# Attention with one product per head: each head on its own half of TensorE's rows, in a fused attention and two-layer expert kernel

## The chip, the core and the metric

The kernel runs on one core of a Trainium2 chip. The metric is device microseconds of one execution; the median of three runs of the kernel before is 1247.96 us (1246.36 to 1250.62). TensorE is called PE here (its weight loads are PEld), VectorE DVE, ScalarE ACT, GpSimd POOL, and SyncE's DMA queue SP.

## What is computed

```python
def _attn_ref(q, k, v, alpha):                       # B, H, S, D = 4, 8, 768, 48
    state = np.zeros((B, H, D, D))
    for t in range(S):
        state = alpha[:, :, t, :, None] * state + np.einsum('bhd,bhe->bhde', k[:, :, t], v[:, :, t])
        y[:, :, t] = np.einsum('bhd,bhde->bhe', q[:, :, t], state)
...
x = attn_out.transpose(0, 2, 1, 3).reshape(3072, 384)
x = _moe_ref(x)      # 8 experts, each token goes to the one with the largest cosine, scaled by its gate
return _moe2_ref(x)  # 4 experts, every token through all of them, mixed by domain_probs
```

All inputs are fp32; a head has 48 numbers per token, and the decay alpha is a number per token and per row of the state.

## The kernel before, in words

**Attention** is done in chunks of 128 tokens, all eight heads of a batch row at a time: 24 units, six to each of the four batch rows, three to each of eight loads. The eight heads stand as four pairs p, a pair on 96 partitions (48 rows for each head). Per load (`g`) and half of the pairs (`pp`), DVE computes with a backward scan the decays from each token to the end of its chunk (`G`, `prep1`), their reciprocals, and with a forward scan the inverse decays (`bf`); POOL multiplies them with q and k (`prep2`), so that `bf` becomes the scaled queries and `G` the scaled keys. `bcall` holds the whole decay of a chunk, once for each head of a pair, with zeros (`hmask`) in the other head's rows. `prep3` on ACT writes the queries twice (`qb`), each time with the other head's 48 rows at zero.

A unit u then runs in three steps of the main loop. `S1(u)`: per pair, one product of the 96 key rows with both masked queries (128x256) gives the scores of two heads in `A`; DVE applies the causal mask (`At`); PE transposes the keys (`kn`). `S2(u)`, a step later: scores times values, per head, into `y` (one head in columns 0 to 63 of the array, the other in 64 to 111); the state `S` of the chunks before, per pair, into the same `y`; and `U`, keys times values per pair (96x96, of which the two 48x48 blocks on the diagonal are wanted). DVE adds `U` to the state and scales it by `bcall` (`state`). `S3(u)`, one more step later: `fin` turns `y` into token rows and router scores; DVE reduces the scores (`raw`), ACT takes squares and a copy (`sj`, `xb`).

**Routing** works on groups of units (`groups`): `choose` (5 DVE instructions), ranks by small products on PE (`route_a`), `route_b` and `route_c` (16 more on DVE), scaling on ACT and an indirect DMA per unit from POOL that scatters token rows to expert rows in DRAM (`xs`). Rows of `xs` that no token fills are zeroed ahead (`prefill`).

**The experts** follow: eight routed ones, then four dense ones, as products in split precision on PE (L120 to L122, L208 to L210, L267 to L269). The order of instructions on each engine is the order in which the code is written, and each engine takes its own in order.

Of the kernel before, what the change touches and what calls it, by code (L numbers as in the profile page):

```python
# [7 lines left out]
F32 = mybir.dt.float32  # L8
# [14 lines left out]
NG = 8  # L23
# [3 lines left out]
W0 = max(WIN)  # L27
NR = 3072
AMIN, BMAX, GMIN = 0.75, 1.0e9, 1.0e-20
# [275 lines left out]
def attention_and_routing(tc, a, small, keep, xs, info_d, wst, load_w, split_w):  # L305
# [3 lines left out]
    ends = [4, 8, 12, 16, 20, 22, 24]  # L309
    groups = list(zip([0] + ends[:-1], ends))  # L310
    with ExitStack() as ctx:
        c1 = ctx.enter_context(tc.tile_pool(name="attc", bufs=1))
        tin = ctx.enter_context(tc.tile_pool(name="tin", bufs=3))
# [4 lines left out]
        xbp = ctx.enter_context(tc.tile_pool(name="xbp", bufs=7))  # L318
# [3 lines left out]
        cst = c1.tile([128, 688], F32, name="cst")  # L322
# [4 lines left out]
        sr = cst[0:1, 608:640].rearrange("p (a e) -> p a e", e=8)  # L327
        tri = keep["ti"][:, 0]
        hmask = c1.tile([96, 2], F32, name="hmask")
        tau = c1.tile([128, 1], F32, name="tau")  # L330
        pre = wst.tile([128, 2 * DM], F32, tag="wraw", name="pre")[:, 0:DM]
        dind = c1.tile([96, 774], F32, name="dind")
        dfw = c1.tile([96, 774], F32, name="dfw")
        bcall = c1.tile([96, NG, 3, 4, 2], F32, name="bcall")
        Sb = [c1.tile([96, 4, 112], F32, name=f"S{j}") for j in range(2)]
        aacc = c1.tile([96, NG, 2], F32, name="aacc")
# [4 lines left out]
        srow = c1.tile([1, 4, 8], BF16, name="srow")  # L341
# [7 lines left out]
        tins, vins, qbd, qqs, kts, mid = {}, {}, {}, {}, {}, {}  # L349
# [11 lines left out]
        def prefill(e):  # L361
            nc.sync.dma_start(
                out=xs[e * NR:e * NR + W0, :].rearrange("(p j) d -> p j d", j=4),
                in_=pre[0:112, :].unsqueeze(1).to_broadcast([112, 4, DM]),
            )
# [5 lines left out]
        def prep1(g, pp, c0=0, c1=3, part=2):  # L371
            al = tins[g, pp]
            lo, hi = 2 * CW * c0, 2 * CW * c1
            if c0 == 0 and part != 1:
                mid[g, pp] = [
                    bd.tile([96, 774], F32, tag="G", name="G"), bd.tile([96, 774], F32, tag="bf", name="bf", bufs=6)
                ]
# [31 lines left out]
        def prep3(g, pp, c0=0, c1=3):  # L409
            qq = qqs[g, pp]  # L410
            if c0 == 0:
                qbd[g, pp] = bd.tile([96, 6, 2, 128], F32, tag="qb", name="qb")
            cs = slice(2 * c0, 2 * c1)
            for s in range(2):
                nc.scalar.activation(  # L415
                    out=qbd[g, pp][:, cs, s, :], in_=qq[:, cs], func=AF.Copy, scale=hmask[:, s:s + 1]
                )

        def prep4(g, pp):
            del mid[g, pp]  # L420
            al = tins.pop((g, pp))[:, 0:774]
            junk = ew.tile([96, 6, 128], BF16, tag="ajunk", name="ajunk", bufs=1)
            nc.scalar.activation(
                out=junk, in_=c3(al, CW)[:, :, 1:CW], func=AF.Relu, scale=-1.0, bias=cbias[0:96, :],
                accum_out=aacc[:, g, pp:pp + 1],
            )
# [3 lines left out]
        def S1(u):  # L430
            g, cl = divmod(u, 3)
            At = wk.tile([128, 8, 128], F32, tag="At", name="At")
            for pp in range(2):
                ps = psA.tile([128, 4, 128], F32, tag="A", name="A")
                kt, qb = kts[g, pp], qbd[g, pp]
                for j in range(2):
                    i = 2 * cl + j
                    nc.tensor.matmul(  # L438
                        ps[:, 2 * j:2 * j + 2, :].rearrange("p s w -> p (s w)"),
                        lhsT=kt[:, i, :], rhs=qb[:, i].rearrange("p s w -> p (s w)"),  # L440
                        start=(j == 0), stop=True, skip_group_check=True,
                    )
                nc.vector.tensor_tensor(  # L443
                    out=At[:, 4 * pp:4 * pp + 4, :], in0=ps,
                    in1=tri.unsqueeze(1).to_broadcast([128, 4, 128]), op=ALU.mult,
                )
            Ats[u] = At
            if u % 6 < 5:
                pk = ps1.tile([128, 4, 96], F32, tag="kn", name="kn")
                for p in range(4):  # L450
                    nc.tensor.matmul(
                        pk[:, p, :], lhsT=kts[g, p // 2][:, 2 * cl + p % 2, :], rhs=ident[0:96, 0:96],
                        is_transpose=True, start=(p == 0), stop=True, skip_group_check=True,
                    )
                kn = wk.tile([128, 4, 96], F32, tag="kn", name="kn_s")
# [4 lines left out]

        def halves(t):
            return bass.AP(t.tensor, t.offset, [t.ap[0], t.ap[1], [64, 2], [1, D]])

        def S2(u):
# [4 lines left out]
            for p in range(4):  # L469
                for s in range(2):  # L470
# [4 lines left out]
                        o, lhsT=v[:, cl, c0:c0 + n], rhs=At[:, 2 * p + s, :],  # L475
# [648 lines left out]
```

## Time and profile before

| | before |
|---|---|
| median of three runs | 1247.96 us |
| the profiled execution, its own time | 1249.04 us |
| its span, first to last instruction | 1247.3 us |
| busy: PE, DVE, ACT, POOL | 95%, 34%, 28%, 26% of the span |
| PE matmuls, weight loads | 6565, 6565 |
| mean granted PE clock | 0.977 of full speed |

The shares are averages over two stages that differ: attention with routing takes about the first 200 us, the experts the remaining 1040 us. PE's 95% is made by the second; in the first, several engines share the work, and the limits are read there stretch by stretch. A matmul of fp32 operands shows as two instructions, each with a weight load.

### The profile page before, as it was taken

The page shows a single profiled execution, that of the slowest core. Times are in us where ns is not written, and L with a number is a line of the kernel's source. Part 1 is how long each engine was busy: PE and PEld are TensorE (multiplying, and loading weights), DVE is VectorE, ACT ScalarE, POOL GpSimd, SP SyncE. Part 2 cuts the span into 40 slices and gives each one's busy share as a digit, 9 for nine tenths or more (in the row PEclk, how much of TensorE's full clock was granted, in tenths as well). Part 3 has the DMA queues.
Part 4 walks back from the last instruction along what each step waited for, and adds up shares of the span by engine and source line. Part 5 has one row for each costly group of instructions (what it writes and reads, how often), then busy time and mean ns, then how long its engine had stood idle before and what let it go on. Part 6 is the DMA issues. An engine that isn't in the chain of part 4 may idle for free.

```text
span 1247.3 us, 16110 instructions
## 1 busy us (share of the span) xinstructions
PE 1189.9 (95%) x6565; PEld 1088.5 (87%) x6565; DVE 424.8 (34%) x791; ACT 351.3 (28%) x624; POOL 321.2 (26%) x223
## 2 busy tenths in 40 slices
PE   5978895999999999999999999999999999999996
PEld 4867785999999999999999999999999899999996
DVE  8998965222222212222222222222212222222221
ACT  3556553444444421111221111131111121111111
POOL 4565644566667510000220000040000020111111
PEclk9997887999999999999999999999999999999998
DMA  8945505444443500000120000030000010000000
GB/s 243 278 150 156 154 31 168 143 131 125 137 137 115 130 26 1 1 1 1 39 64 1 1 1 1 1 93 10 1 1 1 1 39 1 26 26 26 26 26 28
DMA packets 31355, 79.08 MB, mean 63 GB/s; under 512 B 7448, under 2 KB 12824, under 8 KB 29928
## 3 DMA queue, kind: packets, MB, share of 16 engines
q1 hardware_dynamic: 27432, 68.43, 19.0%
q0 software_dynamic: 3840, 9.54, 2.1%
q8 instruction: 53, 0.87, 0.3%
q14 instruction: 30, 0.25, 0.1%
HBM read 62.82 MB, written 15.14 MB: 63 GB/s over the span
## 4 chain that ended last, share of the span: by engine, by line
PE 84%; DVE 7%; issue 4%; DMA 1%; POOL 1%; SPq 0%; ACT 0%; POOLq 0%; ACTq 0%
PE h L120 13%; PE h L122 13%; PE h L121 13%; PE p L269 10%; PE p L268 10%; PE p L267 10%; PE o L208 3%; PE o L209 3%; PE o L210 3%; DVE bf L393 1%; PE A L438 1%; DVE G L380 1%; DVE At L443 1%; PE fin L513 1%; PE xt L175 1%
## 5 line engine op out<-in xcount | busy, mean ns | idle before, releaser
L112 DVE SCALAR_TENSOR_TENSOR hl<-h,hh 128x512 fp32r<-128x512 f32 (+8 forms) x264 | 171.9, 651 | 746.5 <-ACT hh L111 746.5
L68 POOL TENSOR_TENSOR wu<-wraw,wu 128x768 fp32r<-128x768 f32 x96 | 178.3, 1859 | 659.6 <-ACT wu L67 651.4
L111 ACT ACTIVATE hh<-h 128x512 fp32r<-128x512 f32 (+8 forms) x264 | 149.5, 566 | 671.2 <-PE h L122 671.2
L269 PE MATMUL p<-wu,hl 128*128 128x384 f32 x768 | 258.8, 337 | 0.0
L268 PE MATMUL p<-wu,hh 128*128 128x384 f32 x768 | 258.2, 336 | 0.0
L267 PE MATMUL p<-wu,hh 128*128 128x384 f32 x768 | 258.1, 336 | 0.0
L120 PE MATMUL h<-x,wu 128*128 128x512 f32 (+1 forms) x600 | 233.0, 388 | 0.0
L122 PE MATMUL h<-x,wu 128*128 128x512 f32 (+1 forms) x600 | 230.6, 384 | 0.0
L121 PE MATMUL h<-x,wu 128*128 128x512 f32 (+1 forms) x600 | 228.0, 380 | 0.0
L268 PEld LDWEIGHTS p<-wu,hh 128*128 128x128 f32 x768 | 144.3, 188 | 7.4
L267 PEld LDWEIGHTS p<-wu,hh 128*128 128x128 f32 x768 | 144.4, 188 | 7.1
L269 PEld LDWEIGHTS p<-wu,hl 128*128 128x128 f32 x768 | 144.3, 188 | 0.0
L122 PEld LDWEIGHTS h<-x,wu 128*128 128x128 f32 x600 | 112.6, 188 | 26.6
L121 PEld LDWEIGHTS h<-x,wu 128*128 128x128 f32 x600 | 112.8, 188 | 16.1
L120 PEld LDWEIGHTS h<-x,wu 128*128 128x128 f32 x600 | 112.8, 188 | 14.5
L67 ACT ACTIVATE wu<-wraw 128x768 fp32r<-128x768 f32 x96 | 80.8, 843 | 76.2 <-PE o L210 38.1
L280 POOL DMA_INDIRECT out_dram<-acc,toki x24 | 23.4, 973 | 183.4 <-DVE acc L276 178.5
L120 PE MATMUL h<-xh,wu 128*128 128x448 f32 (+6 forms) x192 | 70.2, 365 | 0.0
L438 PE MATMUL A<-qb,G 96*128 96x256 f32 x192 | 55.2, 433 | 14.0 <-ACT qb L415 8.4
L121 PE MATMUL h<-xh,wu 128*128 128x448 f32 (+6 forms) x192 | 68.2, 355 | 0.0
L122 PE MATMUL h<-xl,wu 128*128 128x448 f32 (+6 forms) x192 | 68.0, 354 | 0.0
L208 PE MATMUL o<-hh,wu 128*128 128x448 f32 (+6 forms) x192 | 67.7, 352 | 0.0
(150 smaller groups left out, 1170.6 us busy)
## 6 DMA issues: line engine op xcount, KB each, us to landing
wraw<-in_wu_dram SPq DMA_DIRECT2D x96, 384.0 KB, 3.1
tin<-in_aqk_dram SPq DMA_DIRECT2D x14, 866.6 KB, 6.2
xs<-pre SPq DMA_DIRECT2D x8, 672.0 KB, 9.9
xw<-xs SPq DMA_DIRECT2D x7, 672.0 KB, 6.1
v<-in_v_dram SPq DMA_DIRECT2D x8, 576.0 KB, 6.7
tin<-in_aqk_dram SPq DMA_DIRECT2D x2, 384.0 KB, 6.3
xw<-xs SPq DMA_DIRECT2D x3, 224.0 KB, 3.6
tin<-in_aqk_dram SPq DMA_DIRECT2D x2, 193.5 KB, 4.9
```

The lines of the kernel that those rows point to most:

```text
L67: nc.scalar.activation(out=t[:, 0], in_=r, func=AF.Copy)
L68: nc.gpsimd.tensor_tensor(out=t[:, 1], in0=r, in1=t[:, 0].bitcast(F32), op=ALU.subtract)
L111: nc.scalar.activation(out=hh[:, 0:n], in_=ps, func=AF.Relu)
L112: nc.vector.scalar_tensor_tensor(out=hl[:, 0:n], in0=ps, scalar=0.0, in1=hh[:, 0:n].bitcast(F32), op0=ALU.max, op1=ALU.subtract)
L120: nc.tensor.matmul(ps, lhsT=w[:, 0, ks], rhs=xh(k), start=(k == 0), stop=False)
L121: nc.tensor.matmul(ps, lhsT=w[:, 1, ks], rhs=xh(k), start=False, stop=False)
L122: nc.tensor.matmul(ps, lhsT=w[:, 0, ks], rhs=xl(k), start=False, stop=(k == KD - 1))
L208: nc.tensor.matmul(o, lhsT=w[:, 0, ds], rhs=hh[:, 0:n], start=(f == 0), stop=False)
L267: nc.tensor.matmul(o, lhsT=hh[:, js], rhs=w[:, 0, DM:2 * DM], start=(f == 0), stop=False)
L268: nc.tensor.matmul(o, lhsT=hh[:, js], rhs=w[:, 1, DM:2 * DM], start=False, stop=False)
L269: nc.tensor.matmul(o, lhsT=hl[:, js], rhs=w[:, 0, DM:2 * DM], start=False, stop=(f == NFB - 1))
L438: nc.tensor.matmul(ps[:, 2 * j:2 * j + 2, :].rearrange("p s w -> p (s w)"), lhsT=kt[:, i, :], rhs=qb[:, i].rearrange("p s w -> p (s w)"), ...
```

## The change

A pair now stands on partitions 0 to 47 and 64 to 111 (`R = 112`); the 16 rows between are filled once per buffer from a small array (`pad`), and each load of a pair is two DMAs of 48 partitions instead of one of 96. Every head gets a product of its own on its half of the array's rows, for the scores, for the state's part of `y`, and for `U`. Masked queries (`prep3`), the head mask and the zeroed half of the states go; `bcall` is copied by ACT; the state is 112x4x48. Routing groups are six units, three times, and then three of two; `prefill` writes rows 128 to 447 of each expert instead of 0 to 447.

```diff
+LOW = (NT - sum(WIN) + min(WIN)) // 64 * 64
+R = 112
...
-    ends = [4, 8, 12, 16, 20, 22, 24]
+    ends = [6, 12, 18, 20, 22, 24]
...
-        xbp = ctx.enter_context(tc.tile_pool(name="xbp", bufs=7))
+        xbp = ctx.enter_context(tc.tile_pool(name="xbp", bufs=10))
...
         def load_in(g, pp, lo=0, hi=2311):
             if (g, pp) not in tins:
-                tins[g, pp] = tin.tile([96, 775 + 1536], F32, tag="tin", name="tin")
-            nc.sync.dma_start(out=tins[g, pp][:, lo:hi], in_=a["aqk"][g, pp][:, lo:hi])
+                t = tins[g, pp] = tbuf[(2 * g + pp) % 3]
+                if 2 * g + pp < 3:
+                    nc.sync.dma_start(out=t[D:64, :], in_=a["pad"])
+            for s in range(2):
+                nc.sync.dma_start(
+                    out=tins[g, pp][64 * s:64 * s + D, lo:hi], in_=a["aqk"][g, pp][s * D:s * D + D, lo:hi]
+                )
...
                 nc.vector.reciprocal(c3(dfw, CW)[:, 2 * c0:2 * c1, 0:1], ends_)
-                n = c1 - c0
-                nc.vector.tensor_tensor(
-                    out=bcall[:, g, c0:c1, 2 * pp:2 * pp + 2, :],
-                    in0=ends_.rearrange("p (c a) o -> p c a o", a=2).to_broadcast([96, n, 2, 2]),
-                    in1=hmask.unsqueeze(1).unsqueeze(1).to_broadcast([96, n, 2, 2]), op=ALU.mult,
+                nc.scalar.activation(
+                    out=bcall[:, g, c0:c1, 2 * pp:2 * pp + 2],
+                    in_=ends_.rearrange("p (c a) o -> p c (a o)", a=2), func=AF.Copy,
                 )
...
-        def prep3(g, pp, c0=0, c1=3):
...
-                nc.scalar.activation(
-                    out=qbd[g, pp][:, cs, s, :], in_=qq[:, cs], func=AF.Copy, scale=hmask[:, s:s + 1]
-                )
...
-                for j in range(2):
-                    i = 2 * cl + j
+            ps = [psA.tile([128, 4, 128], F32, tag="A", name=f"A{h}") for h in range(2)]
+            for p in range(4):
+                kt, qq = (x[g, p // 2][:, 2 * cl + p % 2, :] for x in (kts, qqs))
+                for h in range(2):
                     nc.tensor.matmul(
-                        ps[:, 2 * j:2 * j + 2, :].rearrange("p s w -> p (s w)"),
-                        lhsT=kt[:, i, :], rhs=qb[:, i].rearrange("p s w -> p (s w)"),
-                        start=(j == 0), stop=True, skip_group_check=True,
+                        ps[h][:, p, :], lhsT=kt[64 * h:64 * h + D], rhs=qq[64 * h:64 * h + D],
+                        start=(p == 0), stop=True, skip_group_check=True,
                     )
...
                 for p in range(4):
-                    nc.tensor.matmul(
-                        py[:, p, :], lhsT=st[:, p], rhs=qqs[g, p // 2][:, 2 * cl + p % 2, :], start=False, stop=True, skip_group_check=True,
-                    )
+                    qq = qqs[g, p // 2][:, 2 * cl + p % 2, :]
+                    for h in (slice(0, D), slice(64, 64 + D)):
+                        nc.tensor.matmul(
+                            py[h, p, :], lhsT=st[h, p], rhs=qq[h], start=False, stop=True, skip_group_check=True
+                        )
...
                 for p in range(4):
-                    nc.tensor.matmul(
-                        pu[:, p, :], lhsT=kn[:, p, :], rhs=v[:, cl, p * 96:p * 96 + 96],
-                        start=(p == 0), stop=True, skip_group_check=True,
-                    )
+                    for h in (slice(0, 64), slice(64, R)):
+                        c0 = p * 96 + h.start // 64 * D
+                        nc.tensor.matmul(
+                            pu[h, p, :], lhsT=kn[:, p, h], rhs=v[:, cl, c0:c0 + D],
+                            start=(p == 0), stop=True, skip_group_check=True,
+                        )
...
-                    bcv = bcall[:, g2, cl2].unsqueeze(3).to_broadcast([96, 4, 2, D])
+                    bcv = bcall[:, g2, cl2].unsqueeze(2).to_broadcast([R, 4, D])
```

On PE, from the state's products of one unit to the scores of the next, it stood like this before (the state's part of `y`, then `U`, `A` of the next unit, its transposes, and `fin`):

```order
L481 MATMUL y<-bf,S_114 112x128 x4
L491 MATMUL U<-v,kn_s 96x96 x4
L438 MATMUL A<-qb,G 128x256 x4
L451 MATMUL kn<-ti,G 128x96 x4
L513 MATMUL fin<-cst,yt 128x104 x4
```

The same place now, from the last pair of `U` on (`A_388` and `A_389` are the scores of the first and of the second head of a pair):

```order
L485 MATMUL U<-v,kn_s 64x48
L485 MATMUL U<-v,kn_s 48x48
L432 MATMUL A_388<-bf,G 128x128
L432 MATMUL A_389<-bf,G 128x128
L432 MATMUL A_388<-bf,G 128x128
L432 MATMUL A_389<-bf,G 128x128
L432 MATMUL A_388<-bf,G 128x128
L432 MATMUL A_389<-bf,G 128x128
L432 MATMUL A_388<-bf,G 128x128
L432 MATMUL A_389<-bf,G 128x128
L444 MATMUL kn<-ti,G 128x112 x4
```

Four products of 256 columns have become eight of 128, the two heads in turn, and `A` reads `bf` itself where it read the masked copy `qb`.

On DVE, from the update of the state that ends the third step of the main loop to the backward scan in the fourth, it stood like this before:

```order
L504 TENSOR_TENSOR S_113<-U,S_114 96x4x2x48
L505 TENSOR_TENSOR S_113<-S_113,bcall 96x4x2x48
L443 TENSOR_TENSOR At<-A,ti 128x512 x2
L386 RECIPROCAL dfw<-G 96x6
L388 TENSOR_TENSOR bcall<-G,hmask 96x3x4
L393 SCALAR_TENSOR_TENSOR bf<-tin,dfw 96x774
L517 TENSOR_REDUCE raw<-fin 128x8
L380 SCALAR_TENSOR_TENSOR G<-tin,dind 96x774
```

And now (the two scans are the rows with `dfw` and `dind`):

```order
L497 TENSOR_TENSOR S_109<-U,S_110 112x192
L498 TENSOR_TENSOR S_109<-S_109,bcall 112x192
L437 TENSOR_TENSOR At<-A_388,ti 128x512
L437 TENSOR_TENSOR At<-A_389,ti 128x512
L393 RECIPROCAL dfw<-G 112x6
L398 SCALAR_TENSOR_TENSOR bf<-tin_123,dfw 112x774
L510 TENSOR_REDUCE raw<-fin 128x8
L387 SCALAR_TENSOR_TENSOR G<-tin_124,dind 112x774
```

The state's updates have half the elements, and the row of `bcall` ahead of the forward scan is gone; the forward scan now follows the reciprocal.

## Rows read from the trace of the kernel before

**Rows 1.** Busy time by stretch: us from:to, length, busy time of each engine, granted clock, DMA

```profile
25.00:181.00 156.00, 134.26 (x1065) 118.46 (x1064) 136.54 (x255) 89.64 (x189) 91.80 (x61) 0.89 0.55 166
...
207.00:1247.30 1040.30, 1029.10 (x5341) 948.73 (x5340) 249.84 (x408) 244.15 (x398) 209.51 (x136) 1.00 0.15 43
```

**Rows 2.** Timeline of PE: start us, us, instruction; scores of unit 2, transposes

```profile
24.98 0.64 PE L438 MATMUL A<-qb,G 96*128 96x256 f32 x1
...
170.81 0.49 PE L451 MATMUL kn<-ti,G 96*128 96x96 f32 x4
```

**Rows 3.** Timeline of PE at full clock, through the scores of unit 23

```profile
178.28 1.09 PE L474 MATMUL y<-At,v 128*64 128x128 f32 x16
...
179.29 1.13 PE L481 MATMUL y<-bf,S 96*112 96x128 f32 x8
...
180.26 0.84 PE L491 MATMUL U<-v,kn_s 128*96 128x96 f32 x8
...
180.94 1.92 PE L438 MATMUL A<-qb,G 96*128 96x256 f32 x8
...
182.70 1.03 PE L513 MATMUL fin<-cst,yt 112*128 112x104 f32 x8
...
183.66 1.09 PE L474 MATMUL y<-At,v 128*64 128x128 f32 x16
```

**Rows 4.** The chain of waits, in order of time: start us, us, what

```profile
105.14 4.63 DVE bcall L388
...
181.11 1.76 PE A L438 x8
```

**Rows 5.** Groups by line, first 230 us: busy us, mean ns, idle before

```profile
L388 DVE TENSOR_TENSOR bcall<-G,hmask 96x12 f32<-96x12 f32 (+2 forms) x18 | 11.7, 649 | 0.0
```

**Rows 6.** Instructions of L388: count, shortest, median, longest ns

```profile
L388 DVE TENSOR_TENSOR bcall<-G,hmask x18: 127/138/4720, 3.8 to 158.5; 96x12 f32<-96x12 f32 x14, 96x4 f32<-96x4 f32 x2, 96x8 f32<-96x8 f32 x2
```

**Rows 7.** Timeline around the longest of them

```profile
105.05 4.72 DVE L388 TENSOR_TENSOR bcall<-G,hmask 96x12 f32<-96x12 f32 x1
...
107.92 1.81 POOL L68 TENSOR_TENSOR wu<-wraw,wu 128x768 fp32r<-128x768 f32 x1
```

**Rows 8.** Timeline around 31 us: a scan on DVE and a product on POOL

```profile
31.33 1.76 DVE L380 TENSOR_TENSOR_SCAN G<-tin,dind 96x774 f32<-96x774 f32 x1
31.40 3.16 POOL L407 TENSOR_TENSOR G<-tin,G 96x768 f32<-96x768 f32 x1
```

**Rows 9.** Groups by line, first 230 us: states, and a 192-element instruction

```profile
L504 DVE TENSOR_TENSOR S<-U,S 96x384 f32<-96x384 f32 x16 | 8.7, 542 | 9.9 <-PE U L491 9.9
...
L795 DVE TENSOR_TENSOR pv<-ohb,off 128x192 f32<-128x192 bf16 x1 | 0.4, 357 | 0.0
```

**Rows 10.** Groups by line, first 230 us: routing on DVE

```profile
L872 DVE TENSOR_SCALAR gt<-gt 128x4 f32<-128x4 f32 (+1 forms) x7 | 5.6, 805 | 0.2
...
L832 DVE TENSOR_TENSOR sq_g<-sq_g,sq_r 128x4 f32<-128x4 f32 (+2 forms) x8 | 5.4, 675 | 0.3
...
L847 DVE TENSOR_TENSOR key<-raw,mx 128x32 f32<-128x32 f32 (+1 forms) x7 | 5.0, 721 | 0.2
...
L561 DVE TENSOR_SCALAR si<-slotf 128x4 int32<-128x4 f32 (+1 forms) x7 | 4.9, 703 | 0.1
```

**Rows 11.** Timeline: an undisturbed routing instruction on DVE

```profile
121.10 0.17 DVE L550 TENSOR_TENSOR cum<-cum,cs 128x8 bf16<-128x8 bf16 x1
```

**Rows 12.** Timeline of weight loads: the first load of the state's products, idle before in brackets

```profile
179.29 0.93 PEld L481 LDWEIGHTS y<-bf,S 96*112 96x112 f32 x8 [0.17 <-DVE sq_g L831]
```

**Rows 13.** Groups by line, first 230 us: masked queries on ACT

```profile
L415 ACT ACTIVATE qb<-bf,hmask 96x768 f32<-96x768 f32 (+2 forms) x36 | 29.1, 855 | 26.3 <-POOL bf L406 15.4 <-DVE bf L406 10.9
```

**Rows 14.** Timeline of the first 26 us: DMA issues on SP, and DVE waiting for data

```profile
1.65 1.83 SPq L354 DMA_DIRECT2D tin<-in_aqk_dram  x4
...
10.97 0.69 DVE L406 TENSOR_TENSOR bf<-tin,bf 96x512 f32<-96x512 f32 x1 [0.72 <-DMA tin<-in_aqk_dram]
...
25.49 2.16 DVE L380 TENSOR_TENSOR_SCAN G<-tin,dind 96x774 f32<-96x774 f32 x1 [1.59 <-DMA tin<-in_aqk_dram]
```

More of the change, by code (lines that the diff above doesn't have):

```diff
@@ L326, in attention_and_routing @@
         loff = cst[:, 592:608].rearrange("p (a e) -> p a e", e=8)
-        sr = cst[0:1, 608:640].rearrange("p (a e) -> p a e", e=8)
+        sr = cst[0:1, 688:736].rearrange("p (a e) -> p a e", e=8)
         tri = keep["ti"][:, 0]
-        hmask = c1.tile([96, 2], F32, name="hmask")
         tau = c1.tile([128, 1], F32, name="tau")
         pre = wst.tile([128, 2 * DM], F32, tag="wraw", name="pre")[:, 0:DM]
[L332 to L336, printed above, removed]
+        dind = c1.tile([R, 774], F32, name="dind")
+        dfw = c1.tile([R, 774], F32, name="dfw")
+        bcall = c1.tile([R, NG, 3, 4], F32, name="bcall")
+        Sb = [c1.tile([R, 4, D], F32, name=f"S{j}") for j in range(2)]
+        aacc = c1.tile([R, NG, 2], F32, name="aacc")
         half = c1.tile([128, 6], F32, name="half")
@@ L347, in attention_and_routing @@
         inf = keep["inf"]
-        tins, vins, qbd, qqs, kts, mid = {}, {}, {}, {}, {}, {}
+        tbuf = [c1.tile([R, 775 + 1536], F32, name=f"tin{j}") for j in range(3)]
+        tins, vins, qqs, kts, mid = {}, {}, {}, {}, {}
         def load_in(g, pp, lo=0, hi=2311):
             if (g, pp) not in tins:
-                tins[g, pp] = tin.tile([96, 775 + 1536], F32, tag="tin", name="tin")
-            nc.sync.dma_start(out=tins[g, pp][:, lo:hi], in_=a["aqk"][g, pp][:, lo:hi])
+                t = tins[g, pp] = tbuf[(2 * g + pp) % 3]
[5 more added lines that the diff above has]
+                )
         def load_v(g):
@@ L362, in prefill @@
             nc.sync.dma_start(
-                out=xs[e * NR:e * NR + W0, :].rearrange("(p j) d -> p j d", j=4),
-                in_=pre[0:112, :].unsqueeze(1).to_broadcast([112, 4, DM]),
+                out=xs[e * NR + LOW:e * NR + W0, :].rearrange("(p j) d -> p j d", j=4),
+                in_=pre[0:(W0 - LOW) // 4, :].unsqueeze(1).to_broadcast([(W0 - LOW) // 4, 4, DM]),
             )
@@ L607, in attention_and_routing @@
         load_in(0, 0, 0, 259)
-        nc.sync.dma_start(out=hmask, in_=a["hmask"])
         load_in(0, 0, 775, 1287)
@@ L635, in attention_and_routing @@
         prefill(0)
-        load_in(1, 1)
         def fill():
             nc.gpsimd.memset(cum, 0.0)
-            for t in Sb:
-                nc.gpsimd.memset(t, 0.0)
             nc.gpsimd.memset(inf, 0.0)
@@ L690, in attention_and_routing @@
         prep_emb2()
-        prep3(0, 1, 1, 3)
         prep4(0, 0)
+        load_in(1, 1)
         prep4(0, 1)
@@ L708, in attention_and_routing @@
                 load_w(min((i - 3) // 2, NFB))
-            for g in range(1, NG):
-                for pp in range(2):
-                    if 3 * g - 2 + pp == i:
-                        prep3(g, pp)
             if 0 < i < NU:
@@ L805, in attention_and_routing @@
         nc.vector.memset(fl, 0.0)
[L806 to L809 removed]
+        nc.vector.tensor_reduce(out=ft[0:R, 0:1], in_=aacc, op=ALU.max, axis=AX.XY)
+        nc.vector.tensor_scalar(fl[0:R, 0:1], ft[0:R, 0:1], 0.0, None, op0=ALU.is_gt)
+        nc.vector.tensor_reduce(out=ft[0:R, 1:2], in_=bcall.rearrange("r g c p -> r (g c p)"), op=ALU.max, axis=AX.X)
+        nc.vector.tensor_scalar(fl[0:R, 1:2], ft[0:R, 1:2], BMAX, None, op0=ALU.is_gt)
         nc.vector.tensor_tensor(out=num, in0=srt, in1=wins, op=ALU.is_gt)
@@ L1092, in layout @@
         "aqk": aqk,
+        "pad": pad,
         "v": c(v),
```

56 lines of the change are left out of this document (20 added, 36 removed).

## Prediction

> **What bounds the kernel now.** I read the busy time by stretch first. From 207 us to the end PE is busy 1029.1 of 1040.3 us at full clock [rows 1]; the change touches nothing there, so it acts in the first 207 us alone. The stretch from 25 to 181 us holds 21 units: the scores of unit 2 start at 24.98 us [rows 2], those of unit 23 at 180.94 us [rows 3], which is 7.43 us a unit. In it DVE is busy 136.5 of 156 us (88%) and PE 134.3 (86%), PE at a mean granted clock of 0.89 [rows 1]. So two engines share the work almost evenly, and a change has to relieve both to bring its full worth. The chain of waits says which of them ends last: around 105 us it lies on DVE, with 4.63 us in one `bcall` alone; around 181 us, where preparing and routing are nearly done, it lies on PE's scores [rows 4].
>
> PE's own need shows where it isn't kept waiting: from one `y` at 178.28 us to the next at 183.66 us it runs 5.38 us for `y` 1.01, state 0.97, `U` 0.68, scores 1.76 and `fin` 0.96, each from its start to the next one's [rows 3]. With the transposes that unit 23 leaves out, at most 0.49 us [rows 2], a unit takes some 5.8 us. The state's product is the slow form: 8 instructions of 128 columns in 0.97 us, 121 ns each. `y` puts two heads in turn on two halves of the array's columns, and there 16 instructions of the same 128 columns take 1.01 us, 63 ns each: the two halves work side by side [rows 3].
>
> **DVE, part by part.** *`bcall`.* It is taken off DVE, 18 instructions and 11.7 us [rows 5]. But the shortest takes 127 ns and the median 138, the longest 4720 [rows 6]; undisturbed they are worth 18 x 0.138 = 2.5 us, and 9.2 us are waiting. The longest shows for what: it ends 0.04 us after the last POOL product that was under way, at 107.92 + 1.81 = 109.73 us [rows 7]. Does that wait go with it? The forward scan stands right behind and reads two tiles as well, and a scan and a POOL product exclude one another: at 31.33 us a scan of 1.76 us began, and the product that began 0.07 us later took 3.16 us [rows 8]. I therefore let the scan inherit the whole wait and count 2.5 us; the other end is 11.7.
>
> *State.* 36 updates (4 first ones, 16 additions, 16 scalings) go from 384 elements to 192 for a partition. One took 542 ns; an instruction of 192 elements took 357 ns [rows 9]: 36 x 0.185 = 6.7 us.
>
> *Routing.* In the stretch five groups of four units become three of six. A group has 21 DVE instructions of about 0.18 us (the nearest undisturbed row took 0.17 [rows 11]), 3.8 us, or 7.6 for the two that go. Four of the 21 are stretched as `bcall` is: 29 instructions took 20.9 us [rows 10], undisturbed about 4.9, so 16.0 us of waiting over the five groups, 3.2 for each. Two groups fewer save between 0 and 6.4; I take 3.2, since nothing says that all these meetings with POOL recur elsewhere. The new group of two falls into the last units, where the chain is PE's, and costs nothing there; if that cover went, it would cost the same 3.8 us.
>
> Together 2.5 + 6.7 + 7.6 + 3.2 = 20.0 us of 136.5 (ends 16.8 and 32.4). With DVE's idle time of 156 - 136.5 = 19.5 us kept, the stretch would take 136 us.
>
> **PE, part by part.** No row has two products on different halves of the array's rows. *Scores:* 16 instructions of 128 columns for 8 of 256. If the halves work side by side as in `y`, 1.01 us for 1.76; if not, 16 x 121 ns = 1.94. The nearest row is `y` (same count, columns and alternation), so I take 1.01. *State:* the same count and columns, 1.01 for 0.97; the other end is again 1.94. *`U`:* 16 instructions of 48 columns for 8 of 96, between 0.68 (no dearer) and 1.01 (the pace of `y`); I take 0.85. *Changing halves:* at the change from `y` to the state, weight loading stood idle 0.17 us [rows 12]; a unit now has some five such changes instead of two, so 3 x 0.17 = 0.5 us more. The sum: -0.75 + 0.04 + 0.17 + 0.5 = about 0. PE needs 5.8 us a unit as before, 21 x 5.8 = 122 us at full clock, and is not relieved.
>
> At 136 us PE would have to be busy 90% of the time at full clock. Today it idles 21.7 us of the stretch (156 - 134.3), waiting for masks, copies of `y` and routing. I keep 18 of these: 122 + 18 = 140 us, a gain of 16 on the 156.
>
> [...] The scores of the two heads go to two tiles, the two halves of the state's part go to the same `y`. [...]
>
> **The rest.** *ACT* loses 36 masked copies, 29.1 us [rows 13], and gets 18 tiny ones. It was busy 89.6 of 156 us [rows 1], DVE and PE cover it, and I count nothing. *Head:* before the load of `v` SP issues 11 more DMAs (nine second halves, three fills, less `hmask`) at 1.83/4 = 0.46 us each [rows 14]; the first data come two issues later, and the rows that DVE already awaited at 10.97 us (0.72 us) some six issues later, 2.8 us. Against that, the load of (1,1) no longer waits behind the masked copies on ACT, and the 1.59 us that DVE idled at 25.49 us go [rows 14]. I count +0.5 us, between -1.6 and +3. *Prefill* has the same number of DMAs, smaller, off every chain here.
>
> **Sum.** 1249.0 (the profiled execution) - 16 + 0.5 = 1233.5 us. That execution lies 1.1 us above the median of the runs, which takes the forecast to 1232.5; I say 1233. Within 0.3%, 3.7 us, a measurement of this kernel can't tell a difference.
>
> **Rivals.**
> [...]
> 2. *Slower: in neither.* PE needs 5.8 + 1.86 = 7.66 us, 161 us without any waiting, and with 3 us of it 164: +8, about 1257. It decides from 156/21 = 7.43 us of PE a unit on, or from about 6.9 with 10 us of waiting.
> 3. *The waits for POOL vanish with the instructions that showed them.* DVE sheds up to 32.4 us. PE's 122 us and 9 of waiting make 131: a gain of 25, 1224. For it: the chain had 4.63 us in one `bcall`; against it: [rows 8].
> 4. *Nothing:* POOL, which must now issue six scatters in a row between its products, or the later first loads eat the gain: 1248.
>
> **Chances and range.** My forecast 0.55 (its own range 1226 to 1241), rival 1 0.15, rival 2 0.11, rival 3 0.12, rival 4 0.07. Faster by over 0.3%: 0.55 + 0.12 + half of rival 1 = 0.75; within 0.3%: the other half without a little, and most of rival 4, 0.12; slower: rival 2 and the rest, 0.13. From 1221 to 1250 the range leaves out rival 2 and the fast end of rival 3.
>
> **What would show it.** The scores: 16 instructions in about 1.0 us at full clock confirm the pace of `y`, 1.9 refute it; the state's product likewise. The forward scan should now show stretched instances of up to some 4 us; if none appear, rival 3 holds. DVE's busy time from the scores of unit 2 to those of unit 23 should fall from 136.5 to about 116 us, PE's share should rise to 0.9 with a clock above 0.89, and the masked copies be gone without ACT's work ever having been on the chain. The prediction fails if PE takes over 6.4 us a unit, or if DVE waits for the first loads more than 3 us longer.

## The result, and the profile after

The changed kernel takes 1264.12 us (1263.38 to 1266.35), the kernel before, run beside it, 1247.48: ratio 1.0132 (1.0110 to 1.0155), 16.6 us slower where 15 us faster were forecast. The profiled execution took 1263.8 us, its span is 1262.1 us. Its busy time by stretch, beside [rows 1]:

```profile
25.00:181.00 156.00, 127.58 (x1446) 110.60 (x1442) 121.42 (x205) 65.54 (x162) 93.86 (x55) 0.81 0.65 161
222.00:1262.10 1040.10, 1028.91 (x5342) 948.62 (x5340) 249.95 (x408) 244.35 (x399) 209.63 (x136) 1.00 0.15 43
```

The experts are unchanged (1028.9 of 1040.1 us), so all of the loss lies ahead of them. In the stretch TensorE, DVE and ACT are less busy than before, by 7, 15 and 24 us (POOL is busier by 2), and still less got done: the granted clock is 0.81 where it was 0.89. The timeline shows where (start us, us, instruction). First the kernel before (scores of unit 3 and of unit 19, router scores of unit 23, first transpose of the experts), then the changed kernel at the same four places:

```profile
31.82 1.05 PE L438 MATMUL A<-qb,G 96*128 96x256 f32 x4
153.25 1.89 PE L438 MATMUL A<-qb,G 96*128 96x256 f32 x8
191.75 0.18 DVE L517 TENSOR_REDUCE raw<-fin 128x8 f32<-128x32 f32 x1
204.44 1.89 PE L175 MATMUL xt<-ti,xw 112*128 112x112 f32 x8 [0.86 <-DMA xw<-xs]
```

```profile
39.37 1.23 PE L432 MATMUL A<-bf,G 48*128 48x128 f32 x8
155.90 1.16 PE L432 MATMUL A<-bf,G 48*128 48x128 f32 x16
205.82 0.19 DVE L510 TENSOR_REDUCE raw<-fin 128x8 f32<-128x32 f32 x1
219.34 0.98 PE L178 MATMUL xt<-ti,xw 112*128 112x112 f32 x4 [1.76 <-DMA xw<-xs]
```

Up to unit 3 it loses 39.37 - 31.82 = 7.5 us. From unit 3 to 19 it needs 116.5 us instead of 121.4: it gains 4.9 us in 16 units, 0.3 a unit. From unit 19 to the last router scores it needs 49.9 instead of 38.5 us, 11.4 more, and 0.8 behind them. 7.5 - 4.9 + 11.4 + 0.8 = 14.9 us, the difference at the first transpose.

*The head.* DVE waits for data, and the chain of waits in the changed kernel names a load twice (start us, us, what):

```profile
17.89 14.38 DMA tin<-in_aqk_dram
...
55.73 7.92 DMA tin<-in_aqk_dram
```

*TensorE at full clock* (granted 1.00 from 182.00 to 186.60 us; beside [rows 3]; start, us, instruction, one unit):

```profile
182.12 1.16 PE L432 MATMUL A<-bf,G 48*128 48x128 f32 x16
183.21 0.60 PE L444 MATMUL kn<-ti,G 112*128 112x112 f32 x4
183.65 1.05 PE L506 MATMUL fin<-cst,yt 112*128 112x104 f32 x8
184.63 1.09 PE L464 MATMUL y<-At,v 128*64 128x128 f32 x16
185.65 1.08 PE L473 MATMUL y<-bf,S 48*48 48x128 f32 x16
186.66 0.60 PE L485 MATMUL U<-v,kn_s 128*64 128x48 f32 x4
187.75 0.20 PE L485 MATMUL U<-v,kn_s 128*64 128x48 f32 x1 [0.50 <-issue]
188.48 0.25 PE L485 MATMUL U<-v,kn_s 128*64 128x48 f32 x2 [0.52 <-issue]
189.93 0.46 PE L485 MATMUL U<-v,kn_s 128*48 128x48 f32 x4 [1.20 <-issue]
191.35 0.45 PE L485 MATMUL U<-v,kn_s 128*48 128x48 f32 x5 [0.96 <-issue]
191.73 1.65 PE L432 MATMUL A<-bf,G 48*128 48x128 f32 x12
```

From start to start the scores take 1.09 us, `y` 1.02, the state 1.01: the two row halves do work side by side. But the `U` that took 0.6 us in other units takes 5.1 here, with pauses put down to issue (time in which the profile shows nothing that was waited for), and the scores behind it run at a granted clock of 0.50 (from 191.70 to 193.00 us). ACT stands still over the same time: its copy of `y`, ready at 186.7 us, starts at 191.52, again with no instruction that the profile could name as the cause:

```profile
191.52 0.60 ACT L477 ACTIVATE yt<-y 112x512 f32<-112x512 f32 x1 [4.73 <-remote]
```

*DVE* (groups by line, first 230 us, beside [rows 5, 9]), first three rows of the kernel before, then the changed kernel:

```profile
L393 DVE TENSOR_TENSOR_SCAN bf<-tin,dfw 96x774 f32<-96x774 f32 (+2 forms) x18 | 28.5, 1582 | 0.1
L380 DVE TENSOR_TENSOR_SCAN G<-tin,dind 96x774 f32<-96x774 f32 (+2 forms) x18 | 29.9, 1661 | 2.7 <-DMA tin<-in_aqk_dram 2.7
L505 DVE TENSOR_TENSOR S<-S,bcall 96x384 f32<-96x384 f32 x16 | 12.1, 758 | 0.6
```

```profile
L398 DVE TENSOR_TENSOR_SCAN bf<-tin,dfw 112x774 f32<-112x774 f32 (+2 forms) x18 | 34.8, 1935 | 0.6
L387 DVE TENSOR_TENSOR_SCAN G<-tin,dind 112x774 f32<-112x774 f32 (+2 forms) x18 | 33.4, 1856 | 10.0 <-DMA tin<-in_aqk_dram 10.0
L498 DVE TENSOR_TENSOR S<-S,bcall 112x192 f32<-112x192 f32 x16 | 12.1, 759 | 0.6
L497 DVE TENSOR_TENSOR S<-U,S 112x192 f32<-112x192 f32 x16 | 5.6, 350 | 19.1 <-PE U L485 13.3 <-remote 5.8
```

The addition of the state takes 350 ns, as costed. The scaling, which reads two tiles in SBUF, has half the elements and the mean that it had (759 for 758), and the scans went from 1582 to 1935 and from 1661 to 1856: the waits for POOL are still there. The longest scaling took 4.28 us, the shortest 0.36; it starts at 103.96 us, while POOL runs three products in a row, and ends at 108.24, 0.23 us behind the last of them.

### The profile page after: what moved, and what is told of

The parts are those of the page before. It is cut to its first block, busy times and chain, and to the rows that moved or that the text cites. A ratio compares the mean times of both kernels' runs of the same rounds, so it can differ in the third digit from the quotient of the medians.

```text
span 1262.1 us, 17132 instructions
## 1 busy us (share of the span) xinstructions
PE 1188.8 (94%) x7075; PEld 1085.8 (86%) x7075; DVE 410.2 (33%) x752; ACT 328.4 (26%) x605; POOL 324.4 (26%) x220
## 4 chain that ended last, share of the span: by engine, by line
PE 85%; DVE 5%; issue 4%; DMA 3%; POOL 1%; SPq 1%; ACT 0%; another core or an unknown queue 0%; POOLq 0%; DVEq 0%; ACTq 0%
PE h L123 13%; PE h L125 13%; PE h L124 13%; PE p L272 10%; PE p L271 10%; PE p L270 10%; PE o L212 3%; PE o L211 3%; PE o L213 3%; DMA tin<-in_aqk_dram 2%; PE fin L506 1%; PE A L432 1%; DVE bf L398 1%; DVE At L437 1%; PE y L464 1%
## 5 line engine op out<-in xcount | busy, mean ns | idle before, releaser
L70 ACT ACTIVATE wu<-wraw 128x768 fp32r<-128x768 f32 x96 | 80.9, 844 | 80.1 <-PE o L213 38.5
L212 PE MATMUL o<-hl,wu 128*128 128x448 f32 (+6 forms) x192 | 67.6, 352 | 0.0
```

The costliest lines, as they stand in the source:

```text
L70: nc.scalar.activation(out=t[:, 0], in_=r, func=AF.Copy)
L212: nc.tensor.matmul(o, lhsT=w[:, 0, ds], rhs=hl[:, 0:n], start=False, stop=False)
```

## The experiments

| run | what it is | median us | ratio to before |
|---|---|---|---|
| e1 | changed, single loads | 1256.3 | 1.0067 (1.0048 to 1.0086) |
| e2 | before, split loads | 1251.2 | 1.0018 (1.0009 to 1.0028) |
| e3 | changed, old groups | 1259.7 | 1.0100 (1.0082 to 1.0118) |
| e4 | changed, single loads, old groups | 1245.9 | 0.9988 (0.9978 to 0.9997) |
| e7 | e1, third group's scatters a unit later | 1247.4 | 0.9995 (0.9982 to 1.0009) |
| e14 | changed, old prefill | 1254.7 | 1.0057 (1.0039 to 1.0075) |
| e11 | e4, old prefill | 1253.0 | 1.0044 (1.0027 to 1.0061) |
| e17 | e4, prefill halfway | 1255.1 | 1.0058 (1.0041 to 1.0075) |
| e18 | before, short prefill | 1247.2 | 0.9995 (0.9985 to 1.0006) |
| e8 | e4, eight POOL products less | 1244.7 | 0.9977 (0.9967 to 0.9987) |
| e9 | e4, 24 DVE masks more | 1255.5 | 1.0078 (1.0058 to 1.0099) |
| e10 | e4, 16 DVE scalings less | 1246.0 | 0.9987 (0.9976 to 0.9998) |
| e16 | e4, two score buffers | 1251.5 | 1.0024 (1.0012 to 1.0037) |
| e15 | e16 with a free filler | 1252.0 | 1.0031 (1.0017 to 1.0046) |
| e5 | e4, filler behind every `U` | 1249.5 | 1.0017 (1.0007 to 1.0027) |
| e6 | before, filler behind every `U` | 1251.5 | 1.0031 (1.0018 to 1.0043) |
| e12 | e4, filler at the pauses | 1260.8 | 1.0097 (1.0080 to 1.0114) |
| e13 | before, filler at the pauses | 1262.5 | 1.0103 (1.0086 to 1.0119) |

### The loads: e1 and e2

```diff
 # e1: aqk holds 112 rows in DRAM, the 16 between the heads among them
-            for s in range(2):
-                nc.sync.dma_start(
-                    out=tins[g, pp][64 * s:64 * s + D, lo:hi], in_=a["aqk"][g, pp][s * D:s * D + D, lo:hi]
-                )
+            nc.sync.dma_start(out=tins[g, pp][:, lo:hi], in_=a["aqk"][g, pp][:, lo:hi])
 # e2, on the kernel before
-            nc.sync.dma_start(out=tins[g, pp][:, lo:hi], in_=a["aqk"][g, pp][:, lo:hi])
+            for s in range(2):
+                sl = slice(s * D, s * D + D)
+                nc.sync.dma_start(out=tins[g, pp][sl, lo:hi], in_=a["aqk"][g, pp][sl, lo:hi])
```

> The changed kernel, but each load of a pair of heads is one DMA of 112 partitions again (the 16 rows between the heads come with it, so the three fills go too). Theory A, loads: a DMA of 48 partitions is slow for its bytes. After the change a row of 9244 bytes took 753 ns in a DMA engine in the first 60 us, before it 582 ns; then rows should take 580 to 620 ns here, the scores of unit 3 should start at 31 to 34 us instead of 39.4, the wait of 7.92 us for a load at 56 us on the chain should be gone, and the time should fall by 8 to 16 us, to 1248 to 1256 us. Theory B, clock: the loads are a side matter, TensorE's lower granted clock (0.81 against 0.89) from 25 to 181 us eats the gain; then the time falls by 3 us at most, to 1261 or more.

> The kernel before, with nothing changed but each load of 96 partitions split into two DMAs of 48. Theory A: rows of 9244 bytes go from 582 to about 750 ns, DVE waits longer for the load of (1,1) and for a later one, and the kernel gets slower by 5 to 10 us, to 1253 to 1258 us. Theory B: no more than 2 us slower, since eleven issues more cost SyncE 5 us that nothing waits for.

e1 is 7.8 us faster than the changed kernel, its scores of unit 3 start at 32.70 us, not 39.37, and the wait for a load at 56 us is gone from its chain; e2 is 3.0 us slower than the kernel before, between what the two theories said. The first backward scan of load (1,1) on DVE, in the changed kernel, in e1 and in e2:

```profile
32.37 1.77 DVE L387 TENSOR_TENSOR_SCAN G<-tin,dind 112x774 f32<-112x774 f32 x1 [4.42 <-DMA tin<-in_aqk_dram]
```

```profile
25.70 1.77 DVE L382 TENSOR_TENSOR_SCAN G<-tin,dind 112x774 f32<-112x774 f32 x1 [2.06 <-DMA tin<-in_aqk_dram]
```

```profile
27.74 1.77 DVE L382 TENSOR_TENSOR_SCAN G<-tin,dind 96x774 f32<-96x774 f32 x1 [2.67 <-DMA tin<-in_aqk_dram]
```

The transfers themselves got slower, and not their issue: the halves of (1,1) are issued at 17.49 and 17.89 us, before the whole load of the kernel before (19.50), and the second lands at 32.27, where that one landed at 25.47. A row of 9244 bytes occupied a DMA engine for 589 ns on average in the kernel before, 782 in the changed kernel, 683 in e2 and 529 in e1 (mean over the trace's packets of that size). The queues in the first 60 us of the changed kernel and of e1 (KB each, median us from issue to landing):

```profile
DMA packets 5097, 12.82 MB, mean 214 GB/s; under 512 B 1031, under 2 KB 3399, under 8 KB 4487
...
tin<-in_aqk_dram SPq DMA_DIRECT2D x13, 433.3 KB, 10.0
```

```profile
DMA packets 5589, 15.29 MB, mean 255 GB/s; under 512 B 808, under 2 KB 3528, under 8 KB 4840
...
tin<-in_aqk_dram SPq DMA_DIRECT2D x7, 1011.1 KB, 9.5
```

A half of 433 KB, with the other half under way beside it, takes as long as a whole of 1011 KB (10.0 and 9.5 us). That there are two DMAs instead of one is not the whole cause, since e2 has two as well, to partitions 0 to 47 and 48 to 95: a row took 683 ns there and a half of 433 KB 7.9 us, against 782 ns and 10.0 us to partitions 0 to 47 and 64 to 111 in the changed kernel. In one DMA a row took 589 ns to 96 partitions and 529 to 112. In these four kernels the row times differ with the partitions that a DMA writes; why, none of them shows. Of the two theories A is borne out for the changed kernel, with 7.8 us just under its lower bound of 8; 8.8 us of the loss were left.

### Groups and scatters: e3, e4, e7

```diff
 # e3, on the changed kernel; e4, on e1
-    ends = [6, 12, 18, 20, 22, 24]
+    ends = [4, 8, 12, 16, 20, 22, 24]
 # e7, on e1: at i == u1 + 3 the third group is left out, and
+            if i == groups[2][1] + 4:
+                scatter(2)
```

> The changed kernel with the routing groups of before (4, 8, 12, 16, 20, 22, 24). If the new groups of six and the late group of two cost time (later start of a group, six scatters in a row on POOL, one more group in the last units), this is faster by over 3 us, 1261 or less. By the prediction's own term the old groups cost 11 us of DVE time, so up to 1272. If DVE isn't what bounds this stretch, the time stays within 3 us of 1264.

> The changed kernel with single loads of 112 partitions and with the routing groups of before. If the two costs are separate (8 us for the loads, 4.4 for the groups) it takes 1252 us, 1250 to 1254, and what is left over the kernel before, some 4 us, is TensorE's clock and the last units. If the groups only mattered because the loads were late, it stays at 1256.

e3 gains 4.4 us. Together with single loads the old groups are worth 18.3, not 12.2: e4 is at 1245.9. So they are not separate. e1 and e4 run level to unit 19 (148.3 and 147.7 us) and part behind it: the last router scores come at 197.9 and 186.0 us. In e1 TensorE pauses in the same `U` as above, for 4.3 us.

> The changed kernel with single loads, and the six scatters of the third group a unit later. With single loads alone TensorE stands still for 4.5 us within the 16 products of one U (unit 21, at 179 to 184 us), with no wait that the profile shows, while POOL's six scatters run and about 7 us after the last fetch of a block of instructions. If the scatters hold up that fetch, the pause goes from this U or moves with them, and 2 to 4.5 us are gained. If the pause belongs to the fetch alone, it stays in the U of unit 21.

The pause is gone and 8.9 us are gained, more than the 2 to 4.5 expected. That the scatters hold up a fetch of instructions is not shown by it, as e14 tells. Nor are the 8.9 us the scatters' alone: up to unit 20 the two kernels have the same instructions, and yet their scores of unit 13 start at 102.48 us in e1's profiled execution and at 109.10 in e7's. So two executions can lie 6.6 us apart at a place that no edit has touched.

### The prefill: e14, e11, e17, e18

```diff
 # e14, on the changed kernel; e11, on e4 (e17, on e4: LOW = 64)
-LOW = (NT - sum(WIN) + min(WIN)) // 64 * 64
+LOW = 0
 # e18, on the kernel before
-                out=xs[e * NR:e * NR + W0, :].rearrange("(p j) d -> p j d", j=4),
-                in_=pre[0:112, :].unsqueeze(1).to_broadcast([112, 4, DM]),
+                out=xs[e * NR + 128:e * NR + W0, :].rearrange("(p j) d -> p j d", j=4),
+                in_=pre[0:80, :].unsqueeze(1).to_broadcast([80, 4, DM]),
```

> The changed kernel with nothing undone but the prefill (448 rows for each expert again). In the version with single loads and old groups the longer prefill cost 7.2 us, where the trace shows the same times up to unit 10, then a unit at half clock and a forward scan of 7.27 us behind three POOL products. If that is the prefill's own price, it is paid here too: 1269 to 1273. If it was chance of phase (which instructions meet), the time here is anywhere between 1258 and 1272, with other places in the trace.

> The version with single loads and old groups, with the longer prefill of before (448 rows for each expert). By the prediction, off every chain: within 1.5 us of 1245.9. If the shorter prefill made room for the loads, 2 to 5 us slower.

> The version with single loads and old groups, with a prefill of rows 64 to 447: halfway between 1245.9 us (rows 128 to 447) and 1253.0 (rows 0 to 447). If the prefill has a price of its own, about 1249.5, and TensorE's times differ from the first units on. If it only shifts what meets what, anywhere from 1244 to 1255, and the traces part at one place, where a unit falls to half clock or a scan meets POOL.

> The kernel before with nothing changed but the prefill, rows 128 to 447 of each expert as in the change. By the prediction it is off every chain: within 1.5 us of 1248.3. If a prefill of another length only shifts what meets what, the kernel before moves too, by 3 us or more either way, with the traces parting at one place. With the split loads in the kernel before (3 us slower) and the two prefills in the changed kernel (9.5 us apart), this is the last of the pairs that tell how much of a difference here is phase.

The longer prefill makes the changed kernel 9.5 us faster and e4 7.2 us slower, half of it makes e4 9.2 us slower, and in the kernel before its length does nothing (1.2 us, within the noise). e14 lies below both ranges that were expected for it, e11 and e17 above what a price of the prefill would give. Faster in one kernel, slower in another and nothing in the third: the prefill shows no price of its own; it moves what meets what. e14 and the changed kernel issue the same TensorE instructions in the same order. Busy time from 160 to 194 us, and the scores of unit 20, first of e14, then of the changed kernel:

```profile
160.00:194.00 34.00, 33.03 (x426) 29.14 (x425) 24.24 (x92) 19.89 (x48) 20.59 (x17) 0.89 0.20 72
```

```profile
168.11 1.16 PE L432 MATMUL A<-bf,G 48*128 48x128 f32 x16
```

```profile
160.00:194.00 34.00, 28.30 (x297) 24.62 (x297) 18.80 (x61) 14.31 (x35) 19.04 (x14) 0.70 0.10 36
```

```profile
167.43 1.87 PE L432 MATMUL A<-bf,G 48*128 48x128 f32 x14
```

TensorE was granted 0.89 in the one and 0.70 in the other, where it had waited 2.5 us for routing just ahead of these scores; e14's wait there was 0.20 us. From these scores to the next take 5.1 us there and 9.2 here; unit 22 takes 5.1 and 9.6 (the pause, which e14 doesn't have, though its six scatters stand at the same place); from the scores of unit 23 to its router scores 10.1 and 14.1. That is 12.5 us, less the 0.7 that e14 was behind at unit 20: the 11.85 us between their last router scores (193.97 and 205.82 us). The medians are 9.5 us apart: e14's profiled execution was the fastest of its four (1251.6 to 1258.5 us).

How a shift becomes 5 us, for a while, shows where e17 parts from e4, behind the scores of unit 17 (133.3 us in both). DVE and POOL there, first of e4, then of e17:

```profile
134.82 0.34 DVE L492 TENSOR_TENSOR S<-U,S 112x192 f32<-112x192 f32 x1
135.19 0.36 DVE L493 TENSOR_TENSOR S<-S,bcall 112x192 f32<-112x192 f32 x1
...
136.89 1.69 POOL L406 TENSOR_TENSOR bf<-tin,bf 112x768 f32<-112x768 f32 x1
...
138.63 3.40 DVE L825 TENSOR_TENSOR key<-raw,mx 128x32 f32<-128x32 f32 x1
```

```profile
135.88 0.98 POOL L586 DMA_INDIRECT xs<-xb,si  x1 [0.30 <-issue]
135.94 0.36 DVE L492 TENSOR_TENSOR S<-U,S 112x192 f32<-112x192 f32 x1 [1.07 <-PE A L427]
...
136.33 5.84 DVE L493 TENSOR_TENSOR S<-S,bcall 112x192 f32<-112x192 f32 x1
...
136.86 1.70 POOL L406 TENSOR_TENSOR bf<-tin,bf 112x768 f32<-112x768 f32 x1
138.49 1.71 POOL L407 TENSOR_TENSOR G<-tin,G 112x768 f32<-112x768 f32 x1
140.13 1.82 POOL L71 TENSOR_TENSOR wu<-wraw,wu 128x768 fp32r<-128x768 f32 x1
```

POOL has three products in a row, to 141.95 us. The DVE instruction with two SBUF tiles that meets them ends only behind the last, at 142.0 in e4 and 142.2 in e17. Before POOL's run began DVE had done the scaling and two masks in e4, and it did two reductions within it; in e17 it hung on the scaling all the while. Who is stretched shows in the changed kernel too: under three POOL products from 102.94 us on, the addition at 103.56 us, whose one input is in PSUM, took 0.36 us, and the scaling behind it, with two SBUF inputs, 4.28. In what order the two engines go is not settled: the changed kernel's scaling began within the first product; e17's began while a scatter ran on POOL (135.88 to 136.86 us), 0.53 us ahead of the first product, and still waited for all three.

This is not where e17's 9.2 us come from. At unit 19 it is 5.8 us behind e4 (153.51 and 147.70 us), at unit 21 only 0.7 (165.93 and 165.20), since e4 then waits for a mask and for a copy of `y` (17.5 us from the one to the other, 12.4 in e17). The 10.6 us between their last router scores come behind it: 5.8 over units 21 and 22, and 4.1 behind the scores of unit 23, in a wait of ACT that the next part shows.

### What a relief is worth in the middle: e8, e9, e10

```diff
 # e8: first eight weight blocks
-            nc.gpsimd.tensor_tensor(out=t[:, 1], in0=r, in1=t[:, 0].bitcast(F32), op=ALU.subtract)
+            nc.scalar.activation(out=t[:, 1], in_=r, func=AF.Copy)
 # e9
-            for h in range(2):
+            for h in (0, 0, 1):
 # e10
-                        nc.vector.tensor_tensor(out=sn, in0=sn, in1=bcv, op=ALU.mult)
```

> The version with single loads and old groups, but for the eight weight blocks prepared during attention the low part is a plain copy on ACT instead of a subtraction on POOL (the low part is then wrong). Takes eight POOL products of 1.8 us away, with which DVE's instructions collide; DVE's stretched instructions there cost 25 us from the scores of unit 2 to those of unit 23. Theory C: DVE's waits for POOL are what holds this stretch, and a third of them go with a quarter of POOL's products: 4 to 10 us faster than 1245.9, so 1236 to 1242. Rival: the waits move to the next instruction, within 2 us of 1245.9.

> The version with single loads and old groups, with the first head's mask of each unit done twice: 24 more DVE instructions of 0.68 us, 16.3 us of DVE work. If DVE sets the pace alone (my prediction's reading), the time rises by 12 to 16 us, to 1258 or more. If DVE and TensorE set it by turns, by 4 to 10 us. If DVE has become slack, by less than 3.

> The version with single loads and old groups without the scaling of the state (it is left out, and the state with it wrong): 16 DVE instructions of 0.36 us, some 6 us with their waits 9, and a shorter way from U to the next state. If DVE's time counts in full, 6 to 9 us faster than 1245.9; at the rate at which the change's own relief of DVE paid (some 3 us for 9), 2 to 3 us; if DVE is slack, nothing.

e8 gains about 1 us, e9 loses 9.7 for 16.3 us of work, e10 gains nothing for its 6 to 9. These numbers can't be read as the price of DVE's time, since e4, from which they are counted, lacks a pause that the three have. ACT's last copy of `y`, in e4, e8 and e10:

```profile
184.17 0.60 ACT L472 ACTIVATE yt<-y 112x512 f32<-112x512 f32 x1 [0.50 <-PE y L468]
```

```profile
184.36 0.60 ACT L475 ACTIVATE yt<-y 112x512 f32<-112x512 f32 x1 [3.65 <-remote]
```

```profile
185.50 0.60 ACT L472 ACTIVATE yt<-y 112x512 f32<-112x512 f32 x1 [3.63 <-remote]
```

The same pause of 3.6 to 3.8 us, with no cause that the profile names, stands at this copy in e3, e8, e9, e10, e11, e15, e16 and e17, and in no other profiled execution; what makes it stays open. Up to the scores of unit 23, ahead of it, e8 is 3.0 us ahead of e4 (172.95 and 175.91 us), e10 1.8 ahead (174.10) and e9 6.8 behind (182.69). So a relief was worth something there. How much can't be told from these runs: at the same place e17, with an edit that takes nothing from DVE, is 6.6 us behind. That DVE and TensorE bind by turns fits all three, and isn't shown by them.

### The clock: fillers

```diff
 # e5 on e4, e6 on before: 16 behind U; e12 on e4, e13 on before: 32 ahead of fin, 40 ahead of pr
+                nc.tensor.matmul(pub[:, 384:512], lhsT=oneb, rhs=oneb, start=True, stop=True, skip_group_check=True)
 # e16, on e4: one buffer less for the scores
-        psA = ctx.enter_context(tc.tile_pool(name="psA", bufs=3, space=PSUM))
+        psA = ctx.enter_context(tc.tile_pool(name="psA", bufs=2, space=PSUM))
 # e15, on e16: 24 ahead of fin in units 6, 9, 12, 15, 18; 12, 48, 12 ahead of pr
+                nc.tensor.matmul(spare, lhsT=oneb, rhs=oneb, start=True, stop=True, skip_group_check=True)
```

> The same as the run with single loads and old groups, and behind each U sixteen products of 128 bf16 columns of a constant, which nothing reads: TensorE work of about 1 us a unit at full clock that stands just where TensorE waits for DVE. Theory B, clock: the granted clock from 25 to 181 us goes from about 0.83 to over 0.93, the half-clock pieces on the chain (scores 2.0 us, y 1.9, state 1.9) go, and the time falls by 3 to 10 us although work was added. Rival: TensorE's own work sets the pace, so 20 us of work added costs 5 to 20 us. Third: the clock rises and the time stays within 2 us, then half-clock pieces were not what the end waited for.

> The kernel before with the same sixteen products behind each U. There TensorE needs more of its own and was granted 0.89. Theory B: it has less to win and more to lose, 0 to 8 us slower. If the filler helps both kernels alike, the clock doesn't explain the difference between them.

> The version with single loads and old groups, with products of a constant that nothing reads, where TensorE stood idle longest in that version (24.8 us of pauses over 0.7 us between 40 and 186 us): 40 of 128 bf16 columns ahead of each group's rank products, 32 ahead of fin in units 6, 9, 12, 15 and 18. The state's update waits for those behind its own U, as it did in the earlier filler runs, where they stood behind every U and delayed every state by about 1 us. Theory B, clock: the stretch's granted clock goes from 0.89 to 0.95 or more and the time falls by 3 to 9 us, to 1237 to 1243. If half-clock pieces only fill time in which TensorE would wait anyway, the clock rises and the time stays within 2 us of 1245.9. If the fillers stand in the way, over 1248.

> The kernel before with the same filler at the same places. It paused for 18.4 us in all. Theory B: the clock rises from 0.89 to 0.95, and 2 to 6 us are gained. Else within 2 us of 1247.6, or slower where the fillers stand in the way.

> The version with single loads and old groups, with two buffers for the scores instead of three (one for each head). It is the base for the run with the free filler. Between units the first mask is done long before the next scores, so within 2 us of 1245.9.

> The same with filler products that depend on nothing (they write to the PSUM bank that became free, so neither DVE nor TensorE waits for them): 24 of 128 bf16 columns ahead of fin in units 6, 9, 12, 15 and 18, and 12, 48 and 12 ahead of the rank products of the second to fourth group. The earlier fillers were tied to the state: with the filler at the pauses TensorE waited 3.4 to 3.9 us in the filler itself, so those runs told nothing of the clock. Theory B, clock: granted clock over 0.95, and 3 to 8 us faster than the run with two score buffers. Rival: the clock rises and nothing is gained (within 2 us), or the fillers cost what they take, up to 8 us slower.

e5, e6, e12 and e13 tell nothing of the clock: their fillers shared a PSUM tile with `U` (`pub`), so DVE's state waited for them in e5 (around 55 us the products of `U` end at 53.90 us, the fillers at 54.90, and the addition starts at 54.93) and they waited themselves in e12 (3.4 to 3.9 us). The free filler is the test. Busy time from 25 to 181 us, e16, then e15:

```profile
25.00:181.00 156.00, 128.31 (x1502) 110.78 (x1500) 132.04 (x242) 68.05 (x169) 90.36 (x59) 0.81 0.54 169
```

```profile
25.00:181.00 156.00, 135.94 (x1668) 118.29 (x1667) 128.55 (x233) 67.17 (x166) 92.00 (x59) 0.89 0.54 169
```

The clock rises from 0.81 to 0.89, where theory B wanted over 0.95, and the time stays (0.4 us apart). From the scores of unit 2 to those of unit 23 the 192 products of the filler keep TensorE busy for 15.9 us, its other work falls by 4.6 us of busy time (130.2 to 125.6), and the stretch, 158.0 us in e16, is 159.6 in e15: what the clock gave back didn't shorten it. e4 has a clock of 0.90 in the same window without any filler. e16 was expected within 2 us of e4 and came 5.7 us slower, with the pause of ACT, one more sign of how little moves this stretch.

## Why the prediction was wrong, step by step

**Head, +0.5 us (-1.6 to +3): the first step that failed.** It came out at +7.5 us. I counted issues on SP at 0.46 us each and put the transfer at nothing: I let a load of two times 48 partitions land as fast as one of 96. The wait of 1.59 us [rows 14] didn't vanish, it became 4.42 us, and a later load put 7.92 us on the chain. In time the single loads give back 7.8 us (e1).

**TensorE, part by part: right, and cheaper than said.** Scores 1.09 us for the 1.01 taken, state 1.01 for 1.01, `U` 0.59 for 0.85; the 0.5 us for changing halves don't show (the 0.17 us that they were taken from stand in their row as a wait for DVE, `sq_g` [rows 12]), and a unit takes 5.1 us and not 5.8. Side by side in only one of the two products (rival 1) or in neither (rival 2) is refuted: no run shows one row half waiting for the other, and the two halves of the state, which go to one tile `y`, in different partitions of it, need 1.01 us, the pace of its other products (1.02).

**"122 us at full clock": failed.** 21 units of 5.1 us are 108 us, and TensorE was busy for 127.6 in the stretch, at a granted 0.81, for 20 units. I named the clock of 0.89 before and then worked at 1.0. e14 shows what it can decide: 4.1 and 4.0 us in two places, with the same instructions. It isn't the one lever either: e15 raised it from e16's 0.81 and gained nothing.

**DVE: sized too high, and valued wrongly.** Busy time in the stretch fell by 15.1 us (136.5 to 121.4), but over the same 21 units by 12.6 (136.5 to 123.9), where 20 were forecast and 16.8 was the low end. Added up by duration in these units, the state brought 3.0 of its 6.7 us, since its scaling kept its mean of 758 ns. The 10.0 us of `bcall` went and the two scans took 8.1 more, so the inheritance that I assumed holds: the forward scan went to a mean of 1935 ns, with instances of up to 3.4 us. In e4, where the groups are as before, DVE's stretched instructions (those over 0.25 us above the shortest of their form, from the scores of unit 2 to those of unit 23) cost 25.9 us, 28.2 before: `bcall`'s 7.9 went in part to `key` (from 3.7 to 7.8) and the forward scan (none to 1.5). Rival 3 is refuted. But I made 16 us of stretch out of 20 us of DVE. The same 21 units took 153.1 us in e4 (22.86 to 175.91) for 156.0: 2.9 us. With 6.9 us less of DVE's busy time over them (136.5 to 129.7) that is under half; why so little stays open, since the spread between neighbours is larger than what e8 to e10 gained.

**"The new group of two costs nothing" and the last units: failed.** I covered it by TensorE's chain, and there the kernel lost 11.4 us: a pause of 4.5 us in one `U` and two pieces at a granted clock of 0.50 (167.43 to 175.84 us and 191.73 to 200.00), which cost 4.1 and 4.0 us. Both vanish with a prefill of another length (e14) and the pause with later scatters (e7). What makes TensorE and ACT pause stays open: e14 has the same instructions and scatters at the same place, and no pause.

**Rival 4** named the later first loads, with POOL's six scatters, as what could eat the gain, at 0.07, and priced them at the gain itself. They cost more.

So of the 31 us between forecast and result 7 are the head, 7 the middle (from unit 3 to 19 4.9 us were gained; 16/21 of the 16 forecast is 12.2) and some 15 the last units and what follows (12.2 lost where 3 were to be gained); the rest is the forecast gain of unit 2 and what lies between a profiled execution and medians. e4 undoes loads and groups and stands 1.8 us under the kernel before; since e11, e16 and e17, off by one edit that should do nothing, stand at 1251 to 1255, some 4 us of it the pause of ACT, I don't call it a better kernel.

## What to carry to other kernels

Ask of each load what its rows cost on the partitions that it writes: here a row of 9244 bytes took 782 ns in two DMAs of 48 partitions and 529 in one of 112, and to lay the gaps out in DRAM and load the tile whole gave back 7.8 us (e1). Where several engines share a stretch and wait for one another, don't count a relief of one at its size (here 6.9 us of DVE came out as 2.9); work out what the other then needs, at the clock that the trace grants and not at full clock. Where an edit off every chain moves the time by 7 us, compare unit by unit where two traces part, follow them to the end to see whether they meet again, and judge a version by its neighbours as well: a base that lacks a pause which its neighbours have makes every experiment on it look worse.

## What was not expected of the hardware

Two products on different row halves, into one PSUM tile, ran at 63 ns each for 128 columns, as on column halves. One `U` of 16 instructions took 5.1 us (4.9 in e1) instead of 0.6, in bits of one to five with 0.5 to 1.2 us between, in two kernels (changed, e1) and not in a third with the same TensorE instructions (e14). ACT stood still 3.6 to 3.8 us ahead of its last copy of `y` in eight runs, with nothing named that it waited for, and not in e4, e7 or e14. Under POOL's three products in a row a DVE instruction of 0.36 us took 5.84.
